# Attention and mixture of experts: a narrower wait for the first gather, token numbers by group, weight parts spread over tiles

## The chip, the cores and the metric

The kernel runs on one core of a Trainium2 chip. The metric is the device time of one execution in microseconds (us). The engines are named as in the profile: PE (TensorE, matrix products), DVE (VectorE), ACT (ScalarE), POOL (GpSimd) and SP (SyncE, which only issues transfers here). Every engine works through its own instructions in order.

## The reference

Attention in blocks of 64 tokens, over a batch of 8, 8 heads, 576 tokens and a head width of 64, gives x with 4608 rows of 512. A router then picks for each row one of 4 groups and one of the group's 4 experts, and the row goes through that expert's two layers (512 to 1024 to 512), scaled by both softmax weights:

```python
attn = softmax(q_c @ k_c.T / sqrt(64))          # each block of 64 tokens
x = (attn @ v_c) as rows of 8 heads x 64         # 4608 x 512
g_idx = argmax(x @ w_group);  g_w = its softmax weight
e_idx = argmax(x @ w_expert[g_idx]);  e_w = its softmax weight
h = maximum(x @ w1[g, e], 0)
out = g_w * e_w * (h @ w2[g, e])
```

## The kernel before, in words

**Attention stage.** The 4608 rows are 36 tiles of 128 tokens, and the tiles form 9 groups of four. A tile t passes through small stages: `stage_b` (scores on PE), `stage_sub` (row maximum and difference on DVE), `stage_exp` (ACT), `stage_ct` (transposes on PE, a copy on ACT), `stage_pv` (weighted sums on PE), `stage_norm` (DVE divides by the row sum and writes the tile of x) and `stage_xt` (transposes of x for the router). In step t of the main loop `stage_b` works on tile t + 1 and `stage_norm` on tile t - 3.

**Routing and scatter.** After the fourth tile of a group, `route` and `place` work out on DVE, in small pieces strewn between the tiles, the expert, the gate (column D + 1 of x) and the row of each token in a table xs in device memory, which has a section for each expert. One tile's position is worked out in each `stage_norm` (`one_scatter`), and POOL scatters that earlier tile into xs (`scatter_x`, line 752). In the same place POOL writes the token numbers of the present tile (column D) with a small copy from a table of constants. A group's x lies in one of four buffers, taken in turn: the buffer called xl holds groups 0, 4 and 8, so group 8's first tile (tile 32) is written over group 4, whose scatters must have landed.

**The first unit.** After group 3 (GC = 3), `choose` picks the expert with most tokens so far. Its first 256 rows are the first unit of the expert stage, and its weights and rows are fetched during the rest of the attention. `first_loads` (F0 to F5) runs on POOL's queue: F0 and F1 load w1 in two parts (w1r), F2 and F3 gather the 256 rows from xs into xg0 (line 812, 128 rows each), F4 and F5 load w2 in two parts (w2r). `prep_static` (P0 to P7) splits w1 into a rounded part, cast by ACT, and the remainder, subtracted by POOL, 512 columns at a time. P0, P1, P4 and P5 read the first part of w1r, the others the second. R0 and R1 let SP load the next weights into w1r, once these have been read.

**What orders the work.** The order within each engine is written out by hand, in three strings of short names: HEAD, EXTRA (what is added at the end of step t) and TAIL (what follows the loop). A recorder keeps for every operation which boxes of memory it reads and writes and derives the waits between engines: a read waits for earlier writes that overlap, a write for earlier reads and writes. A box is one span of bytes on a range of partitions, from the first to the last byte that an operation touches, so gaps within it count as touched. Transfers have lanes with a semaphore each; scatters of group g use lane s(g mod 4), and a wait for one of a group's scatters is a wait for the last of that group recorded so far. All of xs is one box called "xs": the zero fills of `prefill` write it, scatters are recorded as readers of it (so that they don't wait for each other), and the gathers F2 and F3 are recorded as writers. So a gather waits for all scatters recorded before it (at F2 that includes the first two of group 4), the second gather waits for the first, and a later scatter waits for both.

**Expert stage.** After the attention the units of up to 256 tokens go one by one through the two layers in loops of PE work (lines 1094 and 1109 in the profile), with weights reloaded by SP. POOL sends the last group's scatters (line 1589) once all engines have come to the end of the recorded part; then it gathers the second unit.

Of the kernel before, what the change touches and what calls it, by code (L numbers as in the profile page):

```python
# [1 line left out]

# [10 lines left out]
I32 = mybir.dt.int32  # L13
# [6 lines left out]
P = 128  # L20
# [4 lines left out]
D = H * HD  # L25
# [19 lines left out]

HEAD = "q0 I0 q1 V0 q2 q3 V1 q4 q5 V2 I1 G0 Q3 V3 Q4 V4 Q5 V5 Q6"
EXTRA = {3: "C0", 4: "Z0", 5: "Z1", 6: "Z2", 7: "Z3", 8: "Z4",
         24: "F0", 25: "F1", 27: "P0 P1", 28: "F4", 29: "F2 F3", 30: "P2 P3 F5", 31: "P4 P5 P6"}
TAIL = ("b34 n30 s33 c32 m1 p31 m2 e33 x30 b35 n31 s34 m1 c33 P7 p32 m2 e34 x31 36 n32 s35 B0 c34 p33 17 e35 m1 n33 x32 27 W0"
        " p34 c35 n34 B1 m2 W1 x33 W2 p35 n35 m2 x34 X0 x35 X1 m3 R0 R1 37 18 m3 y0 y1 y2 W3 W4 W5 W6 W7 y3 R2 y4 y5 y6 L0 28 m2 m1 L1 m4 H0 y7"  # L50
        " L2 m5 38 D0 L3 m6 H1 L4 D1 L5")

# [64 lines left out]

class Op:
    def __init__(self, eng, fn, lane):
        self.eng, self.fn, self.lane, self.waits, self.inc = eng, fn, lane, [], False  # L120


class Recorder:
# [28 lines left out]
        hi = lo + sum((n - 1) * abs(st) for st, n in dims[1:]) + 1  # L152
        return p0, p0 + dims[0][1], lo * size, hi * size

    def add(self, eng, fn, reads, writes, lane=None, group=None):
        op = Op(eng, fn, lane)
        op.plain = False
        op.at = len(self.ops[eng])
        need = []
        acc = [(a, False) for a in reads] + [(a, True) for a in writes]  # L160
        boxes = []
        for a, w in acc:
            if isinstance(a, tuple):
                key, b, psum = a[0], a[1], False
            else:
                key, b, psum = self.alias.get(a.tensor.name, a.tensor.name), self.box(a), a.space == PSUM
            boxes.append((key, b, w))
            kept = []
            for o, ob, ow in self.hist.setdefault(key, []):
                over = b[0] < ob[1] and ob[0] < b[1] and b[2] < ob[3] and ob[2] < b[3]  # L170
                if over and o is not op:
                    same = o.lane is None and lane is None and o.eng == eng
                    if same and (eng == "tensor" or not ow):
                        pass
                    elif w or ow or (psum and not same):
                        need.append(o)
                if over and w and b[0] <= ob[0] and b[1] >= ob[1] and b[2] <= ob[2] and b[3] >= ob[3] and o is not op:
                    continue
                kept.append((o, ob, ow))
            self.hist[key] = kept  # L180
        for key, b, w in boxes:
            self.hist[key].append((op, b, w))
        if lane is not None:
            n, gen = self.lanes.get(lane, (0, None))
            if group is None or group != gen:
                need += self.last_of(lane)
                self.lanes[lane] = (n + 1, group)
                op.gen = [op]
            else:
                self.lanes[lane] = (n + 1, gen)  # L190
                op.gen = self.live[lane][-1].gen
                op.gen.append(op)
            self.live.setdefault(lane, []).append(op)
            op.number = n + 1
        self.want(op, need)
        self.ops[eng].append(op)
        op.clock = dict(self.seen[eng])
        return op
# [62 lines left out]
    def play(self, name, eng):  # L261
        for op in self.ops[name]:
# [2 lines left out]
                eng.wait_ge(*self.wait(*w))  # L265
            if op.fn is None:
                continue
            z = op.fn(eng)
            for w in last:
                z._wait_ge(*self.wait(*w))  # L270
            if op.lane is not None:
# [19 lines left out]
class Engine:  # L291
    def __init__(self, rec, name):
        self.rec, self.name = rec, name

    def do(self, fn, reads=(), writes=(), lane=None, group=None):
        return self.rec.add(self.name, fn, list(reads), list(writes), lane, group)

    def __getattr__(self, op):
        def f(*args, **kw):
# [6 lines left out]
                writes, reads = [args[0]], aps(args[1:]) + aps(named.values())  # L306
            reads = [a for a in reads if a.space != DRAM]
            writes = [a for a in writes if a.space != DRAM]
            z = self.do(lambda e: getattr(e, op)(*args, **named), reads, writes, lane, group)  # L309
            z.plain = True  # L310
            return z
        return f
# [3 lines left out]
def moe_kernel(tc, qk, v, wgs, w1, w2, cst, out):  # L316
# [4 lines left out]
    with ExitStack() as ctx:  # L321
# [114 lines left out]
        with ExitStack() as c1:  # L436
# [132 lines left out]
            def stage_norm(t):  # L569
# [9 lines left out]
                g, i = divmod(t, NG)  # L579
                if i == 0:  # L580
                    st["x", g] = xl if g % 4 == GL % 4 else xbufs[g % 4 - 1]
                R.gpsimd.tensor_copy(st["x", g][:, i, D:D + 1].bitcast(I32), cs[:, C_TID + t:C_TID + t + 1])
                x = st["x", g][:, i, 0:D]
                R.vector.tensor_tensor(out=x.rearrange("p (h x d) -> p x h d", x=2, d=HD), in0=o[..., 0:HD],
                                        in1=rc.unsqueeze(3).broadcast_to([P, 2, 4, HD]), op=ALU.mult)
# [164 lines left out]
            def scatter_x(pos, g, i):  # L750
                x = st["x", g][:, i, :]
                R.gpsimd.do(lambda e: e.indirect_dma_start(xs, bass.IndirectOffsetOnAxis(ap=pos, axis=0), x, None),  # L752
                            [pos, x, ("xs", (0, 1, 0, 1))], [], "s%d" % (g % 4), g)

            def one_scatter():

# [41 lines left out]
            def first_loads(i):  # L798
# [10 lines left out]
                elif i < NP + 2:  # L809
                    j = i - NP  # L810
                    number(("r", j), xi0[0:1, j:j + 1], E * RE * P)
                    R.gpsimd.do(lambda e: e.dma_start(xg0[:, j, :], xs[ds(st["r", j], P), :]), [], [xg0[:, j, :], ("xs", (0, 1, 0, 1))], "g%d" % j)
                else:
                    load2(R.gpsimd, lambda: st["e0"], i - NP - 2)

# [49 lines left out]

            def prefill(j):
                i = (E * RE, 0, 1, 2, 3)[j]
                R.sync.do(lambda e: e.dma_start(xs[i * P:(i + 1) * P, :], pad), [pad], [("xs", (0, 1, 0, 1))], "z%d" % j)

            def reload(i):  # L870
                (load1, load2)[i // NP](R.sync, 0, i % NP)
# [800 lines left out]
```

## Time and profile before

| | us |
|---|---|
| three runs | 624.0, 624.8, 625.17 |
| median | 624.8 |
| the profiled execution | 627.61 |
| its span, first to last instruction | 626.0 |

| engine | busy us | share of the span |
|---|---|---|
| PE | 583.8 | 93% |
| DVE | 364.3 | 58% |
| ACT | 263.1 | 42% |
| POOL | 161.2 | 26% |

A row of the trace gives the start in us, a length in us, the engine, the line, the operation, what it writes and what it reads with the shapes, and how many alike were merged (x2). Brackets hold the idle time of the engine ahead of it and what ended that time. Operations that go through the recorder all carry line 309, that of the recorder's helper, and are told apart by their operands. SPq is the queue of SP's transfers. PEclk is the granted clock of TensorE as a share of full speed; 0.50 is 1.2 GHz and 1.00 is 2.4 GHz. An indirect transfer of POOL shows there with the time of its issue only; its way to memory is in the chain as a DMA.

### The profile page before, as it was taken

How to read it: one execution, taken by the hardware profiler on the slowest of the kernel's cores; microseconds unless marked ns; L12 is line 12 of the kernel's file. 1: busy time of each engine (PE TensorE's matmuls, PEld its weight loads, DVE VectorE, ACT ScalarE, POOL GpSimd, SP SyncE). 2: the span in 40 equal slices, each digit the busy share in tenths (PEclk: the TensorE clock that was granted, in tenths of full speed). 3: DMA queues.
4: the chain of work that ended last, by engine and by line, in shares of the span. 5: the costliest groups of instructions: out<-in, count | busy, mean ns of one | idle time of the engine just before them, and what ended most of it. 6: DMA issues, size and time to landing. Idle time of an engine off the chain costs nothing.

```text
span 626.0 us, 16004 instructions
## 1 busy us (share of the span) xinstructions
PE 583.8 (93%) x5711; PEld 503.1 (80%) x5712; DVE 364.3 (58%) x688; ACT 263.1 (42%) x367; POOL 161.2 (26%) x279
## 2 busy tenths in 40 slices
PE   6897989957899999989999999999999999999995
PEld 4766767745779799878889899989989988898984
DVE  4586769863876672127497674725525578854311
ACT  2464445743444461125475362625215365552111
POOL 0002324348342311221333212221111124311120
PEclk9798889985999999999999999999999999999999
DMA  8987997729639984115489954451712686931110
GB/s 299 422 278 258 372 363 229 228 77 286 173 108 323 328 300 171 68 30 200 142 298 339 301 191 180 171 206 63 281 50 89 238 317 206 339 102 67 34 38 30
DMA packets 43103, 128.24 MB, mean 205 GB/s; under 512 B 4590, under 2 KB 4974, under 8 KB 41136
## 3 DMA queue, kind: packets, MB, share of 16 engines
q1 hardware_dynamic: 32192, 93.93, 43.4%
q0 software_dynamic: 10864, 33.64, 15.3%
q8 instruction: 35, 0.57, 0.4%
q14 instruction: 12, 0.10, 0.0%
HBM read 106.40 MB, written 21.93 MB: 205 GB/s over the span
## 4 chain that ended last, share of the span: by engine, by line
PE 77%; DMA 10%; DVE 5%; issue 4%; POOL 2%; SPq 1%; ACT 1%; POOLq 0%; ACTq 0%; DVEq 0%
PE banks L1109 29%; PE banks L1094 22%; PE banks L309 14%; PE banks L1078 5%; DMA xs<-xl,pos 3%; DMA w1r<-in_moe_w_dram 2%; DMA xgr<-xs 2%; PE banks L994 2%; DMA out_dram<-xl,io__154 1%; DMA qk<-in_qk_dram 1%; PE banks L1040 1%; PE banks L1063 1%; PE banks L1010 1%; DVE big L309 1%; DVE m L309 1%
## 5 line engine op out<-in xcount | busy, mean ns | idle before, releaser
L1094 PE MATMUL banks<-big,w1h 128*128 128x256 f32 x896 | 128.1, 283 | 1.6 <-issue 1.6
L1094 PEld LDWEIGHTS banks<-big,w1h 128*128 128x128 f32 x896 | 117.3, 192 | 3.0 <-issue 2.0
L1255 ACT ACTIVATE big<-banks 128x512 fp32r<-128x512 f32 x58 | 34.5, 597 | 158.6 <-PE banks L1094 105.3
L1109 PE MATMUL banks<-big,big 128*128 128x512 f32 x360 | 84.6, 393 | 0.0
L1585 POOL DMA_INDIRECT out_dram<-xl,io__154 x37 | 41.1, 1111 | 154.8 <-DVE xl L1321 144.0
L1109 PEld LDWEIGHTS banks<-big,big 128*128 128x128 f32 x360 | 66.5, 188 | 14.4 <-ACT big L1305 0.7
L1354 DVE SCALAR_TENSOR_TENSOR big<-banks,big 128x512 fp32r<-128x512 f32 x54 | 36.1, 687 | 64.5 <-ACT big L1255 64.1
L1094 PE MATMUL banks<-big,w1l 128*128 128x256 f32 x448 | 72.3, 283 | 0.6 <-DVE w1l L1331 0.6
L1109 PE MATMUL banks<-w2h,big 128*128 128x512 f32 x288 | 71.2, 393 | 1.5 <-ACT big L1255 1.4
L1331 DVE TENSOR_TENSOR w1l<-w1r,w1h 128x2048 fp32r<-128x2048 f32 x28 | 63.1, 2290 | 16.1 <-ACT w1h L1242 14.3
L1321 DVE TENSOR_SCALAR xl<-banks,io__154 128x512 f32<-128x512 f32 x33 | 24.7, 748 | 67.5 <-PE banks L1109 66.0
L1109 PEld LDWEIGHTS banks<-w2h,big 128*128 128x128 f32 x288 | 53.1, 188 | 13.0 <-ACT big L1255 1.8
L1094 PEld LDWEIGHTS banks<-big,w1l 128*128 128x128 f32 x448 | 61.9, 192 | 0.8 <-DVE w1l L1331 0.8
L1242 ACT CAST w1h<-w1r 128x2048 fp32r<-128x2048 f32 x28 | 52.1, 1903 | 6.7 <-DMA w1r<-in_moe_w_dram 4.9
L309 PE MATMUL banks<-va,pT 64*64 64x65 f32 x1152 | 30.0, 247 | 13.9 <-DVE x L309 6.9
L309 PEld LDWEIGHTS banks<-va,pT 64*64 64x64 f32 x1152 | 24.2, 154 | 23.2 <-DVE x L309 7.9
L309 PE MATMUL banks<-qk 64*64 64x64 f32 x1152 | 29.4, 233 | 11.6 <-issue 7.8
L309 PEld LDWEIGHTS banks<-qk 64*64 64x64 f32 x1152 | 23.0, 141 | 20.2 <-issue 11.0
L1335 DVE TENSOR_TENSOR w2l<-w2r,w2h 128x1024 fp32r<-128x1024 f32 x32 | 37.1, 1218 | 1.8 <-ACT w2h L1274 1.2
L309 ACT COPY pT<-banks 128x512 f32<-128x512 f32 x36 | 21.1, 585 | 36.4 <-PE banks L309 35.8
L1109 PE MATMUL banks<-w2l,big 128*128 128x512 f32 x144 | 35.6, 389 | 0.0
L752 POOL DMA_INDIRECT xs<-x,pos x24 | 24.8, 1033 | 39.7 <-DVE pos L309 27.0
(218 smaller groups left out, 898.6 us busy)
## 6 DMA issues: line engine op xcount, KB each, us to landing
w1r<-in_moe_w_dram SPq DMA_DIRECT2D x30, 1024.0 KB
w2r<-in_moe_w_dram SPq DMA_DIRECT2D x30, 1024.0 KB
qk<-in_qk_dram SPq DMA_DIRECT2D x15, 1024.0 KB, 15.3
xgr<-xs POOLq DMA_DIRECT2D x38, 257.0 KB, 5.2
va<-in_v_dram SPq DMA_DIRECT2D x24, 390.0 KB
qk<-in_qk_dram SPq DMA_DIRECT2D x6, 512.0 KB, 8.6
w1r<-in_moe_w_dram POOLq DMA_DIRECT2D x2, 1024.0 KB, 9.7
w2r<-in_moe_w_dram POOLq DMA_DIRECT2D x2, 1024.0 KB, 7.2
```

Of the source, the lines that this page charges most:

```text
L309: z = self.do(lambda e: getattr(e, op)(*args, **named), reads, writes, lane, group)
L752: R.gpsimd.do(lambda e: e.indirect_dma_start(xs, bass.IndirectOffsetOnAxis(ap=pos, axis=0), x, None), [pos, x, ("xs", (0, 1, 0, 1))], [], ...
L1078: m = pe.matmul(ph[n], a_[:, c, 0:P], w_[:, c, n * 512:(n + 1) * 512], start=(i == 0), stop=(i == 11))
L1094: m = pe.matmul(ph[f // 2][:, f % 2 * 256:f % 2 * 256 + 256], w_[:, c, f * P:(f + 1) * P], a_[:, c, :], start=(i == 0), stop=(i == 11))
L1109: m = pe.matmul(py[j], a_[:, f, half[j]], w_(b, f), start=(i == 0), stop=(i == 23))
L1242: lambda b, s, j: ac.copy(wt[b][0][:, s], w1r[j]), K1)
L1255: ac.activation(hth()[:, 2 * b:2 * b + 2, :], ph[b].rearrange("p (f t) -> p f t", f=2), AF.Relu).then_inc(S["Ha"], 1)
L1321: return ve.tensor_scalar(out=yb[:, j, :], in0=py[j], scalar1=io_[:, j, 1:2], scalar2=None, op0=ALU.mult)
L1331: lambda b, s, j: ve.tensor_sub(wt[b][1][:, s], w1r[j], wt[b][0][:, s].bitcast(F32)), K1, js)
L1335: m = ve.tensor_sub(wt[b][4 + 2 * j + i], w2r[j][:, 2 * i:2 * i + 2], wt[b][2 + j][:, 2 * i:2 * i + 2].bitcast(F32))
L1354: ve.scalar_tensor_tensor(out=htl()[:, 2 * b:2 * b + 2, :], in0=ph[b].rearrange("p (f t) -> p f t", f=2), scalar=0.0, in1=hth()[:, 2 * b:2 ...
L1585: gp.indirect_dma_start(out, bass.IndirectOffsetOnAxis(ap=io[:, j, 0:1].bitcast(I32), axis=0), yb[:, j, :], None, bounds_check=N - 1, oob_ ...
```

## The change

The first unit's gathers wait only for the scatters of groups 0 to 3 (`after=`), as nothing later writes their rows. For this "xs" is replaced by two names: "zeros", for the fills, which scatters still wait for, and "rows", under which each group's scatters are found. The gathers don't write either, so they don't wait for each other and later scatters don't wait for them. Token numbers are copied by POOL for four tiles at once, at the first tile of a group: 9 copies of 128x4 in place of 36 of 128x1. The box of such a copy goes from column D of the first tile to column D of the fourth, and so covers x of the second to fourth tile. The parts P0 to P7 are dealt out one to a tile in EXTRA and TAIL, and F4 now follows P1. The other lines give each recorded operation its own line number in the profile.

```diff
--- before.py
+++ after.py
@@ -1,3 +1,4 @@
+import sys
 from contextlib import ExitStack
 
 import numpy as np
@@ -45,8 +46,8 @@
 
 HEAD = "q0 I0 q1 V0 q2 q3 V1 q4 q5 V2 I1 G0 Q3 V3 Q4 V4 Q5 V5 Q6"
 EXTRA = {3: "C0", 4: "Z0", 5: "Z1", 6: "Z2", 7: "Z3", 8: "Z4",
-         24: "F0", 25: "F1", 27: "P0 P1", 28: "F4", 29: "F2 F3", 30: "P2 P3 F5", 31: "P4 P5 P6"}
-TAIL = ("b34 n30 s33 c32 m1 p31 m2 e33 x30 b35 n31 s34 m1 c33 P7 p32 m2 e34 x31 36 n32 s35 B0 c34 p33 17 e35 m1 n33 x32 27 W0"
+         24: "F0", 25: "F1", 27: "P0", 28: "P1 F4", 29: "F2 F3 P2", 30: "P3 F5", 31: "P4"}
+TAIL = ("b34 n30 s33 c32 m1 p31 m2 e33 x30 P5 b35 n31 s34 m1 c33 p32 m2 e34 x31 P6 36 n32 s35 B0 c34 p33 17 e35 m1 n33 x32 P7 27 W0"
         " p34 c35 n34 B1 m2 W1 x33 W2 p35 n35 m2 x34 X0 x35 X1 m3 R0 R1 37 18 m3 y0 y1 y2 W3 W4 W5 W6 W7 y3 R2 y4 y5 y6 L0 28 m2 m1 L1 m4 H0 y7"
         " L2 m5 38 D0 L3 m6 H1 L4 D1 L5")
 
@@ -117,7 +118,7 @@
 
 class Op:
     def __init__(self, eng, fn, lane):
-        self.eng, self.fn, self.lane, self.waits, self.inc = eng, fn, lane, [], False
+        self.eng, self.fn, self.lane, self.waits, self.inc, self.stage = eng, fn, lane, [], False, None
 
 
 class Recorder:
@@ -152,11 +153,11 @@
         hi = lo + sum((n - 1) * abs(st) for st, n in dims[1:]) + 1
         return p0, p0 + dims[0][1], lo * size, hi * size
 
-    def add(self, eng, fn, reads, writes, lane=None, group=None):
+    def add(self, eng, fn, reads, writes, lane=None, group=None, after=()):
         op = Op(eng, fn, lane)
         op.plain = False
         op.at = len(self.ops[eng])
-        need = []
+        need = list(after)
         acc = [(a, False) for a in reads] + [(a, True) for a in writes]
         boxes = []
         for a, w in acc:
@@ -265,7 +266,8 @@
                 eng.wait_ge(*self.wait(*w))
             if op.fn is None:
                 continue
-            z = op.fn(eng)
+            with self.tc.nc.source_location(__file__, op.line):
+                z = op.fn(eng)
             for w in last:
                 z._wait_ge(*self.wait(*w))
             if op.lane is not None:
@@ -292,8 +294,10 @@
     def __init__(self, rec, name):
         self.rec, self.name = rec, name
 
-    def do(self, fn, reads=(), writes=(), lane=None, group=None):
-        return self.rec.add(self.name, fn, list(reads), list(writes), lane, group)
+    def do(self, fn, reads=(), writes=(), lane=None, group=None, line=None, after=()):
+        z = self.rec.add(self.name, fn, list(reads), list(writes), lane, group, after)
+        z.line = line or sys._getframe(1).f_lineno
+        return z
 
     def __getattr__(self, op):
         def f(*args, **kw):
@@ -306,7 +310,7 @@
                 writes, reads = [args[0]], aps(args[1:]) + aps(named.values())
             reads = [a for a in reads if a.space != DRAM]
             writes = [a for a in writes if a.space != DRAM]
-            z = self.do(lambda e: getattr(e, op)(*args, **named), reads, writes, lane, group)
+            z = self.do(lambda e: getattr(e, op)(*args, **named), reads, writes, lane, group, sys._getframe(1).f_lineno)
             z.plain = True
             return z
         return f
@@ -579,7 +583,7 @@
                 g, i = divmod(t, NG)
                 if i == 0:
                     st["x", g] = xl if g % 4 == GL % 4 else xbufs[g % 4 - 1]
-                R.gpsimd.tensor_copy(st["x", g][:, i, D:D + 1].bitcast(I32), cs[:, C_TID + t:C_TID + t + 1])
+                    R.gpsimd.tensor_copy(st["x", g][:, :, D].bitcast(I32), cs[:, C_TID + t:C_TID + t + NG])
                 x = st["x", g][:, i, 0:D]
                 R.vector.tensor_tensor(out=x.rearrange("p (h x d) -> p x h d", x=2, d=HD), in0=o[..., 0:HD],
                                         in1=rc.unsqueeze(3).broadcast_to([P, 2, 4, HD]), op=ALU.mult)
@@ -750,7 +754,7 @@
             def scatter_x(pos, g, i):
                 x = st["x", g][:, i, :]
                 R.gpsimd.do(lambda e: e.indirect_dma_start(xs, bass.IndirectOffsetOnAxis(ap=pos, axis=0), x, None),
-                            [pos, x, ("xs", (0, 1, 0, 1))], [], "s%d" % (g % 4), g)
+                            [pos, x, ("zeros", (0, 1, 0, 1)), ("rows", (g, g + 1, 0, 1))], [], "s%d" % (g % 4), g)
 
             def one_scatter():
 
@@ -809,7 +813,8 @@
                 elif i < NP + 2:
                     j = i - NP
                     number(("r", j), xi0[0:1, j:j + 1], E * RE * P)
-                    R.gpsimd.do(lambda e: e.dma_start(xg0[:, j, :], xs[ds(st["r", j], P), :]), [], [xg0[:, j, :], ("xs", (0, 1, 0, 1))], "g%d" % j)
+                    R.gpsimd.do(lambda e: e.dma_start(xg0[:, j, :], xs[ds(st["r", j], P), :]), [], [xg0[:, j, :]], "g%d" % j,
+                                after=[o for o, b, _ in R.hist["rows"] if b[0] <= GC])
                 else:
                     load2(R.gpsimd, lambda: st["e0"], i - NP - 2)
 
@@ -865,7 +870,7 @@
 
             def prefill(j):
                 i = (E * RE, 0, 1, 2, 3)[j]
-                R.sync.do(lambda e: e.dma_start(xs[i * P:(i + 1) * P, :], pad), [pad], [("xs", (0, 1, 0, 1))], "z%d" % j)
+                R.sync.do(lambda e: e.dma_start(xs[i * P:(i + 1) * P, :], pad), [pad], [("zeros", (0, 1, 0, 1))], "z%d" % j)
 
             def reload(i):
                 (load1, load2)[i // NP](R.sync, 0, i % NP)
```

## Rows read from the trace of the kernel before

**Rows 1.** The table of stretches (us; busy time and instructions of each engine, granted clock, DMA).

```profile
100.00:125.00 25.00, 23.67 (x617) 18.17 (x611) 22.71 (x80) 16.53 (x37) 10.61 (x15) 1.00 0.83 257
...
125.00:150.00 25.00, 13.74 (x268) 9.55 (x261) 14.03 (x42) 8.33 (x18) 16.24 (x21) 0.72 0.50 156
...
300.00:626.00 326.00, 318.09 (x1985) 284.65 (x1984) 179.30 (x198) 134.15 (x150) 77.01 (x140) 1.00 0.49 174
...
155.00:156.00 1.00, 1.00 (x23) 0.67 (x25) 0.70 (x4) 1.00 (x4) 0.69 (x2) 0.50 0.97 386
...
54.00:56.00 2.00, 2.00 (x42) 1.55 (x38) 1.09 (x6) 0.85 (x3) 0.00 (x0) 0.50 0.96 209
...
56.00:58.00 2.00, 2.00 (x42) 1.85 (x42) 1.33 (x3) 0.78 (x2) 0.35 (x1) 0.69 0.88 225
```

**Rows 2.** The chain that ended last, 117 to 157 us (start, us, what).

```profile
117.25 8.31 DMA xs<-xl,pos
...
126.24 3.32 DMA xg0r<-xs
...
133.89 1.03 POOL xs L752
...
138.60 7.12 DMA xs<-xl,pos
...
147.97 9.34 PE banks L309 x100
```

**Rows 3.** POOL in order of time (start, us, engine, line, operation; idle before and releaser).

```profile
112.33 2.51 POOL L309 TENSOR_TENSOR w1l<-w1r,w1h 128x512 fp32r<-128x512 f32 x2 [3.19 <-ACT w1h L309]
...
116.14 0.81 POOL L418 DMA_DIRECT2D w2r<-in_moe_w_dram  x1
...
126.24 0.57 POOL L812 DMA_DIRECT2D xg0r<-xs  x1 [7.77 <-DMA xs<-xl,pos]
...
134.93 0.19 POOL L309 CAST x<-cs 128x1 int32<-128x1 f32 x1
...
172.75 0.96 POOL L1589 DMA_INDIRECT xs<-xl,pos  x1 [4.43 <-PE banks L309]
```

**Rows 4.** VectorE (DVE) in order of time.

```profile
100.94 0.24 DVE L309 TENSOR_TENSOR one<-lg,mx 128x80 f32<-128x80 f32 x1
...
113.64 1.29 DVE L309 TENSOR_TENSOR one<-lg,mx 128x80 f32<-128x80 f32 x1
...
118.78 0.17 DVE L309 TENSOR_TENSOR x<-gt 128x4 f32<-128x4 f32 x1
...
124.69 0.69 DVE L309 TENSOR_TENSOR x<-banks,rc 128x512 f32<-128x512 f32 x1
...
135.15 2.43 DVE L309 TENSOR_TENSOR x<-gt 128x4 f32<-128x4 f32 x1 [3.06 <-POOL x L309]
...
141.39 0.23 DVE L309 TENSOR_TENSOR ps<-banks,oh 128x64 f32<-128x64 f32 x1 [1.22 <-PE banks L309]
...
145.81 0.69 DVE L309 TENSOR_TENSOR xl<-banks,rc 128x512 f32<-128x512 f32 x1 [4.06 <-DMA xs<-xl,pos]
...
157.79 0.69 DVE L309 TENSOR_TENSOR xl<-banks,rc 128x512 f32<-128x512 f32 x1
```

**Rows 5.** TensorE (PE) in order of time.

```profile
52.33 0.34 PE L309 MATMUL banks<-qk 64*64 64x64 f32 x6 [1.99 <-issue]
...
126.27 0.70 PE L309 MATMUL banks<-va,pT 64*64 64x65 f32 x32
...
138.24 1.15 PE L309 MATMUL banks<-va,pT 64*64 64x65 f32 x32 [5.85 <-DVE x L309]
```

**Rows 6.** ScalarE (ACT) and SP's DMA queue in order of time.

```profile
111.62 1.14 ACT L309 CAST w1h<-w1r 128x512 fp32r<-128x512 f32 x2
...
142.29 6.89 SPq L412 DMA_DIRECT2D w1r<-in_moe_w_dram  x2
```

## The prediction

> **What bounds the kernel now.** I read the table of stretches first, the chain that ended last second, and then GpSimd (POOL), VectorE (DVE) and TensorE (PE) instruction by instruction between 100 and 160 us. The table [rows 1] parts the kernel in two. From 300 us on PE is busy for 318 of 326 us at full clock: the expert stage is bound by PE, and nothing in this diff touches its code. In the attention stage it is DVE that is nearly full (22.7 of 25 us in 100 to 125). The odd stretch is 125 to 150: PE works 13.7 of 25 us at a mean clock of 0.72, DVE 14 of 25, and DMA halves. Some 12 us of work is missing there, and the question is who holds it up.
>
> The chain [rows 2] names the holder. At 117.25 POOL issues a scatter of tokens (xl to xs), and the chain runs through its landing (8.3 us), then the first unit's gather (3.3 us), then the next scatter at 133.89, then one at 138.60 that takes 7.1 us to land, and then PE work at a slow pace. POOL's own rows [rows 3] say it outright: the gather of line 812 stood 7.77 us for that scatter, that is from 118.47, and the next scatter began at 133.89 only, so POOL, which works in order, was held for 15.4 us. 14.3 us of it is waiting (7.77, then the first gather's landing, then the second's); the rest is the issue of the two gathers.
>
> DVE's rows [rows 4] show the two places where this reaches the attention. The write of the gates of group 6, 0.17 us at 118.78 for the group before, waits 3.06 us at 135.15 for POOL's copy of a token number and then takes 2.43 us. The write of tile 32 into xl waits 4.06 us at 145.81 for the landing of the scatter of 138.60, because xl still holds group 4. PE [rows 5] idles 5.85 us for the first of these; after that its clock falls to 0.50 (1.2 of 2.4 GHz): the mean of 0.72 over 125 to 150 makes 14 us at half, 155 to 156 is still at 0.50 [rows 1], and thirty-two matmuls take 1.15 us where they took 0.70.
>
> **The change part by part.** I set the sum in the profiled execution: it took 627.61 us, its span 626.0, and the median of the runs is 624.8, 0.45% below it. I take the saving off the median.
>
> *The wait of the gather.* The first gather now needs scatters of groups 0 to 3 alone. The last of these stands ahead of P0 on POOL, so it was issued before 112.33 [rows 3], and landing takes 7 to 8.3 us [rows 2]: it is there by 120.6 at the latest, about when the gathers come; the second gather no longer waits for the first, nor the next scatter for both. Removed from POOL: 14.3 us. What that is worth stands with those who waited:
> (a) The gates of group 6: 3.06 us of waiting, and 2.43 less 0.17 for the slow write, 5.3 us.
> (b) Tile 32: 4.05 us. Group 4's last scatter should be issued near 125 (below) and land by 133, while tile 32 comes at about 136.6 (145.81 less 5.3, 4.05, 1.2 and 1.05, plus the 2.4 of (d)), a cover of some 3 us. If that cover is gone, at most these 4.05 us come back.
> (c) The clock. The chain's 9.34 us of PE work from 147.97 ran at half clock; at 0.70 to 1.15 it is 5.7 us, a gain of 3.6. Of the stretch before, DVE's wait of 1.22 us for PE at 141.39 goes as well: 1.2. Together 4.8, and nothing if the clock stays down.
>
> *The low parts, one to a tile.* Eight casts on ACT (0.57 us each) and eight subtractions on POOL (1.25 us each) stay the same [rows 3, 6]; P1 moves one tile on and ahead of F4, P2 comes into the tile of the gathers and right behind them, P3 stays ahead of F5, and P4 to P7 spread over later tiles. On ACT there is room: no cast stands on the chain. On DVE something is won: its operation of 113.64 took 1.29 us instead of 0.24 [rows 4] while POOL ran P0 and P1 back to back, from 112.33 to 114.84; with P0 alone POOL is through at 113.6, so (f) 1.05 us. The two slow rows show that such a DVE operation, both of whose inputs lie in SBUF, stands until POOL's subtraction ends. Between the ends 0 and 1.05 I take 1.05, since DVE starts it after POOL would be through. SP's two reloads of w1 wait for P5 and P7; they were issued from 142.29 over 6.89 us [rows 6], so the second near 149. By the count below P5 ends near 135 and P7 near 143, both earlier, so they cost nothing; DMA is at 0.50 there.
>
> *The token numbers.* 36 copies of 0.19 us on POOL become 9. That is nothing by itself, since POOL idles. But the group's copy spans the rows between the tiles, so DVE, which didn't wait for a copy in its tile writes, now waits for it in the second to fourth tile of each group, and the copy sits in POOL's queue. For groups 0 to 6 POOL is early. For group 7 I count the queue, with 1.2 us for a scatter, 1.25 for a subtraction, 0.8 for a weight load (F4, F5) and 0.75 for a gather [rows 2, 3]: P0 ends 113.6, the scatter in tile 25's step 114.8, P1 (its cast a tile later on ACT, 115.4) 116.65, F4 117.45, scatter 118.65, two gathers 120.15, P2 121.4, scatter 122.6, P3 123.85, F5 124.65, scatter 125.85, copy 126.05. The positions, which DVE works out ahead of each tile, come earlier and don't hold it. DVE writes tile 29 at 124.69 [rows 4], less (f) 123.65. So (d) a new wait of 2.4 us, between 0 (POOL's gaps shorter, the cast earlier) and 4 (register loads before the gathers not hidden). Behind it on DVE stand the maximum and subtraction of tile 32, on PE the weighted sum of tile 30. (e) The copy of group 8 stands behind P6 and a scatter; tile 33 waits 0 to 1.25 us for it, I take 0.6.
> (g) PE then idles some 1.5 us. A pause of 1.99 us before 52.33 [rows 5] was followed by a clock of 0.50 in 54 to 56 and 0.69 in 56 to 58 [rows 1]; these 3 us at half clock cost 1.5, and I take half of it, 0.7.
>
> *The rest.* The line numbers given to instructions add none. The end of attention carries to the end of the kernel: the last scatters (172.75) wait 4.43 us for PE [rows 3], the first unit's and the second's loads follow those, and PE is full after. Sum: 5.3 + 4.05 + 4.8 + 1.05 - 2.4 - 0.6 - 0.7 = 11.5 us, 624.8 to 613.3. With every bound on the good side (no d, e, g) it is 15.2, 609.6; with d 4, e 1.25, g 1.5 and no f it is 7.4, 617.4.
>
> **The rivals.**
> *The clock stays down.* The new wait idles PE at 126 as the old one did at 133, and PE is fed slowly enough that the clock remains at half as it did up to 156 us [rows 1]. For: the pause of 1.99 us was enough. Against: there it was back within some 3 us, since PE was fed. Price: the 4.8 us of (c) and 0.7 more, 613.3 + 5.5 = 618.8.
> *The wait is not lifted.* If the gather is still held (by the lane it shares with group 4, or by another transfer), the same 14.3 us fall on POOL ahead of group 7's copy, for which DVE now waits: the copy comes at 140.4, tile 29 then, tile 32 three tiles of 3.3 us later at 150.3 instead of 145.81, and the 12.0 us from there to tile 35 (157.79) stay: 4.5 us slower, 629.3. It decides from a copy of group 7 later than 126.05 + 11.5 = 137.5. Against: lane counts of groups 0 to 3 are below group 4's, and a wait for a constant count passes once that is reached.
> *Collisions.* Two DVE operations were stopped by POOL's subtractions, for 1.05 and 2.26 us [rows 4]; the forecast has none. One subtraction a tile can meet the routing of groups 5 to 8 in all of them: eight times 1.05 instead of none gives 613.3 + 8.4 = 621.7. Against: each tile has a few such small operations in 3.3 us, most DVE work reads PSUM and ran on undelayed beside POOL. The Trainium skill (SBUF — State Buffer, section SBUF: two separate sides) speaks against the change here: the port pair is an exclusive lock, held for the whole instruction, against DVE operations with two SBUF inputs and also in its two-port modes; by that, up to 8 x 1.25 = 10 us could be lost as an estimate. The two rows agree on the lock, and no row shows a two-port case.
> *Hidden anyway.* Loads, not POOL, would set the end of attention: no change, 624.8. Against: DMA at 0.50 in 125 to 150.
>
> **How the numbers follow.** Forecast 0.70, clock 0.15, collisions 0.06, not lifted 0.06, hidden 0.03. A measurement of this kernel can tell about 0.2% (1.2 us) from no change. Faster: 0.70 + 0.15 + 0.06 = 0.91; same 0.03; slower 0.06. The range runs from every bound good (609.6, set 609.0) over the forecast's bad end to the clock's case (618.8, set 619.0), and leaves out collisions, slower, hidden: 0.15.
>
> **What would show it.** Right: both gathers issued near 119 to 120 without a DMA wait, group 4's last scatter by 126, no DVE wait for a DMA at tile 32, 125 to 150 with DVE above 20 us busy; tile 35 near 146; a DVE wait for POOL's copy at tile 29 of 1 to 4 us. Wrong: a DMA wait at line 813's gathers, a wait at tile 29 above 6 us, a clock of 0.5 for over 5 us, or an expert stage whose start doesn't move with tile 35.

## The result, and the profile of the changed kernel

The changed kernel takes 618.3 us (median of five runs, 616.05 to 620.83), the kernel before 625.17 in the runs beside it (624.0 to 626.44): a ratio of 0.9877, with a 95% interval of 0.9848 to 0.9907. The profiled execution took 618.3 us with a span of 616.7, 9.3 us less than the profiled one of before. The forecast was 613.3 in a range of 609.0 to 619.0, so the first measurement lies 0.7 us inside the range's upper end.

Lines have moved: 756 is the scatter of a tile, 816 the gathers, 586 the copy of token numbers, 438 POOL's subtraction of w1's low part, 588 DVE's write of a tile of x, 577 its reading of the row sums ahead of that, 705 the write of the gates, 662 the difference called `one`, 1594 the last group's scatters; on PE 534 are the scores, 570 the weighted sums, 600 the transposes of a tile of x, 824 the transposes of the first unit. The table of stretches first, against [rows 1]:

```profile
100.00:125.00 25.00, 22.25 (x529) 17.13 (x522) 20.35 (x75) 15.44 (x34) 13.13 (x16) 0.93 0.95 274
125.00:150.00 25.00, 19.18 (x414) 14.50 (x413) 16.92 (x66) 15.65 (x31) 15.94 (x17) 0.96 0.73 205
150.00:175.00 25.00, 24.12 (x168) 20.00 (x167) 18.77 (x74) 12.31 (x16) 10.38 (x8) 0.90 0.47 155
```

The stretch of 125 to 150 has filled up: PE 19.2 us busy for 13.7, DVE 16.9 for 14.0, the clock 0.96 for 0.72, DMA 0.73 for 0.50. But 100 to 125 now holds a stretch at half clock (0.93 for 1.00), and 150 to 175 still does, at 0.90; before, its row was this:

```profile
150.00:175.00 25.00, 22.96 (x224) 20.70 (x225) 16.47 (x69) 13.15 (x24) 11.58 (x14) 0.88 0.68 193
```

POOL's own rows, against [rows 3]:

```profile
117.16 1.00 POOL L756 DMA_INDIRECT xs<-xl,pos  x1 [0.30 <-DVE gt L702]
118.16 1.15 POOL L816 DMA_DIRECT2D xg0r<-xs  x2
121.65 1.27 POOL L438 TENSOR_TENSOR w1l<-w1r,w1h 128x512 fp32r<-128x512 f32 x1 [2.33 <-ACT w1h L437]
...
126.89 1.01 POOL L756 DMA_INDIRECT xs<-xl,pos  x1 [0.30 <-DVE pos L765]
127.89 0.21 POOL L586 CAST x<-cs 128x4 int32<-128x4 f32 x1
...
164.70 0.97 POOL L1594 DMA_INDIRECT xs<-xl,pos  x1 [6.00 <-PE banks L428]
```

Both gathers go out in one piece at 118.16, right behind a scatter, without a wait for a DMA; before, POOL stood 15.4 us here. Group 4's last scatter begins at 126.89, not at 138.60. DVE, against [rows 4]:

```profile
112.93 0.36 DVE L662 TENSOR_TENSOR one<-lg,mx 128x80 f32<-128x80 f32 x1
...
123.27 0.69 DVE L588 TENSOR_TENSOR x<-banks,rc 128x512 f32<-128x512 f32 x1
...
128.13 0.69 DVE L588 TENSOR_TENSOR x<-banks,rc 128x512 f32<-128x512 f32 x1 [1.27 <-POOL x L586]
...
134.51 0.16 DVE L705 TENSOR_TENSOR x<-gt 128x4 f32<-128x4 f32 x1
...
137.94 0.69 DVE L588 TENSOR_TENSOR xl<-banks,rc 128x512 f32<-128x512 f32 x1
...
140.99 0.69 DVE L588 TENSOR_TENSOR xl<-banks,rc 128x512 f32<-128x512 f32 x1 [0.62 <-POOL xl L586]
...
147.79 0.17 DVE L577 TENSOR_SCALAR rc<-banks 128x8 f32<-128x8 f32 x1 [1.49 <-PE banks L824]
...
148.24 0.69 DVE L588 TENSOR_TENSOR xl<-banks,rc 128x512 f32<-128x512 f32 x1
```

These are `one`, tile 28, tile 29 with the new wait for the group's copy, the gates of group 6 (no wait, 0.16 us), tile 32 (no wait for a DMA), tile 33 with its new wait, and tile 35 at 148.24, where it came at 157.79. PE shows where the clock was lost instead, against [rows 5]:

```profile
116.33 0.38 PE L534 MATMUL banks<-qk 64*64 64x64 f32 x9 [2.36 <-issue]
...
118.23 1.15 PE L570 MATMUL banks<-va,pT 64*64 64x65 f32 x32
...
148.99 1.12 PE L600 MATMUL banks<-cs,xl 128*128 128x128 f32 x4 [2.37 <-DVE xl L588]
```

PE paused 2.36 us within a series of matmuls that waits for nothing the profile shows (it calls such time "issue"), and thirty-two matmuls then took 1.15 us, the half-clock price; it idled 2.37 us ahead of tile 35's transposes, and four of them took 1.12 us where four take 0.60 to 0.66 at full clock.

From the starts of the same instructions in both traces, four spans add up to the 9.3 us:

| us | before | after | saved |
|---|---|---|---|
| start to tile 28 (DVE's write) | 121.47 | 123.27 | -1.80 |
| tile 28 to tile 35 | 36.32 | 24.97 | 11.35 |
| tile 35 to the last group's scatters | 14.96 | 16.46 | -1.50 |
| from there to the end of the span | 453.25 | 452.00 | 1.25 |

### The profile page after: what moved, and what is told of

It reads as the page before. It is cut to its first block, busy times and chain, and to the rows that moved or that the text cites. A ratio compares the mean times of both kernels' runs of the same rounds, so it can differ in the third digit from the quotient of the medians.

```text
span 616.7 us, 15975 instructions
## 1 busy us (share of the span) xinstructions
PE 580.7 (94%) x5711; PEld 500.1 (81%) x5712; DVE 361.0 (59%) x688; ACT 263.6 (43%) x367; POOL 157.6 (26%) x252
## 4 chain that ended last, share of the span: by engine, by line
PE 82%; DMA 6%; issue 4%; DVE 4%; POOL 1%; ACT 1%; SPq 1%; DVEq 0%; ACTq 0%; POOLq 0%
PE banks L1114 29%; PE banks L1099 24%; PE banks L1083 5%; PE banks L570 4%; PE banks L534 3%; PE banks L600 3%; PE banks L558 3%; DMA w1r<-in_moe_w_dram 2%; PE banks L999 2%; PE banks L620 2%; DMA qk<-in_qk_dram 1%; PE banks L1045 1%; DMA xs<-x,pos 1%; PE banks L1068 1%; PE banks L1015 1%
## 5 line engine op out<-in xcount | busy, mean ns | idle before, releaser
L1336 DVE TENSOR_TENSOR w1l<-w1r,w1h 128x2048 fp32r<-128x2048 f32 x28 | 63.1, 2290 | 16.1 <-ACT w1h L1247 14.3
L1114 PE MATMUL banks<-w2l,big 128*128 128x512 f32 x144 | 35.6, 390 | 0.0
L1584 POOL COPY in__155<-xgr 128x2 int32<-128x2 int32 x22 | 10.8, 490 | 88.9 <-PE banks L999 75.4
L1340 DVE TENSOR_TENSOR big<-w2r,big 128x1024 fp32r<-128x1024 f32 x28 | 32.5, 1220 | 1.5 <-ACT big L1251 1.5
```

The source lines that it names most:

```text
L1114: m = pe.matmul(py[j], a_[:, f, half[j]], w_(b, f), start=(i == 0), stop=(i == 23))
L1336: lambda b, s, j: ve.tensor_sub(wt[b][1][:, s], w1r[j], wt[b][0][:, s].bitcast(F32)), K1, js)
L1340: m = ve.tensor_sub(wt[b][4 + 2 * j + i], w2r[j][:, 2 * i:2 * i + 2], wt[b][2 + j][:, 2 * i:2 * i + 2].bitcast(F32))
```

## The experiments

Theory: the narrow wait carries the whole gain, the other two parts move nothing by themselves, and what the forecast lacks is the clock. Rivals: a part of the gain is the line numbers'; the new copies' waits eat a part of it; the spread subtractions carry a part of it; the late end of attention is set at tile 35, by something the change brought. The kernels ran in three sets, each on a chip of its own beside the kernel before: line numbers, wait, copies, and wait with spread in the first (before: 623.97 us); spread, wait with copies, the change again and the exact boxes in the second (624.69); the rest in the third (618.62). All of them carry the change's line numbers. First each part alone.

### Line numbers alone

```diff
+            with self.tc.nc.source_location(__file__, op.line):
+                z = op.fn(eng)
```

> The kernel before with one line number per recorded operation and nothing else. Both theories: no change, 625 us within 0.2%, and a second profile of before. If the profile of before (627.61) was at the slow end of its executions, this one shows a span nearer 623.5, with the same two waits (gates of group 6, tile 32) but a shorter stay at half clock. If line numbers matter, it moves by over 1.2 us.

622.22 us (618.96 to 626.18), ratio 0.9966 (0.9941 to 0.9992). No engine has another instruction, so a third of a per cent is what two builds of the same work can differ by here; the 0.2% that the prediction named as the bound of a measurement was too fine. The two kernels below that keep the old wait carry the line numbers too and are not faster than before (1.0033 and 1.0002), so no part of the gain is seen to be theirs. Of the kernel before, 22 of 23 runs lie between 617.93 and 626.27 in this set. The waits of before stand in DVE's rows of this kernel:

```profile
132.89 2.43 DVE L705 TENSOR_TENSOR x<-gt 128x4 f32<-128x4 f32 x1 [1.90 <-POOL x L586]
...
144.26 0.69 DVE L588 TENSOR_TENSOR xl<-banks,rc 128x512 f32<-128x512 f32 x1 [4.76 <-DMA xs<-xl,pos]
```

### The narrow wait alone

(The zero fills write "zeros" too, as in the change.)

```diff
-                            [pos, x, ("xs", (0, 1, 0, 1))], [], "s%d" % (g % 4), g)
+                            [pos, x, ("zeros", (0, 1, 0, 1)), ("rows", (g, g + 1, 0, 1))], [], "s%d" % (g % 4), g)
...
-                    R.gpsimd.do(..., [], [xg0[:, j, :], ("xs", (0, 1, 0, 1))], "g%d" % j)
+                    R.gpsimd.do(..., [], [xg0[:, j, :]], "g%d" % j,
+                                after=[o for o, b, _ in R.hist["rows"] if b[0] <= GC])
```

> Only the gather's wait is narrowed; copies and subtractions as before. Theory A (the wait carries nearly all of the gain): by POOL's queue the last scatter of group 4 is issued near 126.4 and lands by 134, before tile 32, and no DVE wait for POOL's copy at tile 29 is left: 616.5 to 618.5 us, as fast as the whole change. Rival B (without the spreading, P4 to P6 in a row hold POOL and the gain is halved): 620.5 to 622.5 us.

613.81 us (612.31 to 616.35), ratio 0.9833 (0.9807 to 0.9859): the whole gain, not less than with the rest, and 2.7 us below the better of the two times expected. Beside the kernel with line numbers alone it is 8.4 us. With the subtractions still bunched, POOL no longer waits, and P4 to P6 now run into DVE's routing. POOL's row, DVE's rows and PE's row of this kernel, one after the other:

```profile
126.12 3.72 POOL L438 TENSOR_TENSOR w1l<-w1r,w1h 128x512 fp32r<-128x512 f32 x3
```

```profile
126.38 3.57 DVE L662 TENSOR_TENSOR one<-lg,mx 128x80 f32<-128x80 f32 x1
129.87 0.23 DVE L664 TENSOR_TENSOR ls<-lg,mx 128x80 f32<-128x80 f32 x1
```

```profile
131.51 0.70 PE L570 MATMUL banks<-va,pT 64*64 64x65 f32 x32 [3.36 <-DVE x L588]
```

The operation, 0.24 us long where nothing stops it, starts 0.26 us after the first of three subtractions and ends as the third does (126.12 + 3.72 = 129.84; the next row of DVE starts at 129.87), and PE idles 3.36 us for it. Yet tile 35 comes at 145.90.

### The grouped copies alone

```diff
-                R.gpsimd.tensor_copy(st["x", g][:, i, D:D + 1].bitcast(I32), cs[:, C_TID + t:C_TID + t + 1])
...
+                    R.gpsimd.tensor_copy(st["x", g][:, :, D].bitcast(I32), cs[:, C_TID + t:C_TID + t + NG])
```

> Only the copies are grouped; the gather waits as before. Theory A: group 7's copy stands behind the held gathers and the scatter of tile 28's step, at about 139.6, and DVE stands at tile 29 from 124.7 until then; tile 32 comes near 150 instead of 145.8: 629 us (627 to 631), slower. Rival (the copies are off every path): 625 us.

625.89 us (622.25 to 627.74), ratio 1.0033 (1.0005 to 1.0061); 3.7 us above the kernel with line numbers alone. This is the prediction's slow rival in a kernel of its own: the old wait on POOL, with group 7's copy behind it. The wait came as expected, the time did not (629). DVE's row of tile 29, then PE's next one:

```profile
135.72 0.69 DVE L588 TENSOR_TENSOR x<-banks,rc 128x512 f32<-128x512 f32 x1 [15.39 <-POOL x L586]
```

```profile
136.46 1.15 PE L570 MATMUL banks<-va,pT 64*64 64x65 f32 x32 [13.91 <-DVE x L588]
```

Tile 29 waits 15.39 us, PE idles 13.91. It costs so little more than before because the waits at the gates and at tile 32 are then over (tile 32 at 147.72 without a wait): one long wait takes the place of two short ones.

### The spread subtractions alone

```diff
-         24: "F0", 25: "F1", 27: "P0 P1", 28: "F4", 29: "F2 F3", 30: "P2 P3 F5", 31: "P4 P5 P6"}
+         24: "F0", 25: "F1", 27: "P0", 28: "P1 F4", 29: "F2 F3 P2", 30: "P3 F5", 31: "P4"}
```

(and P5 to P7 in TAIL, as in the change)

> Only the subtractions are spread; the gather waits and the copies go as before. Theory A (POOL is held by the gathers, and the scatter of tile 28's step has the same work ahead of it): 622 to 624 us, no change. Rival (spreading is worth its relief on DVE even so): 620 to 621 us.

624.12 us (622.77 to 628.44) beside 624.69, ratio 1.0002 (0.9974 to 1.003): nothing that could be measured. `one` takes 0.36 us here too, but another operation of the routing (0.17 us elsewhere) now stands until a subtraction of POOL (128.61 to 129.89) is through, and both old waits are there in DVE's rows:

```profile
128.42 1.50 DVE L703 TENSOR_TENSOR cum<-cum 128x16 bf16<-128x16 bf16 x1
...
133.17 1.22 DVE L705 TENSOR_TENSOR x<-gt 128x4 f32<-128x4 f32 x1 [3.10 <-POOL x L586]
...
141.76 0.69 DVE L588 TENSOR_TENSOR xl<-banks,rc 128x512 f32<-128x512 f32 x1 [3.19 <-DMA xs<-xl,pos]
```

### The narrow wait with one other part

The change with the copies put back to one a tile (the reverse of the diff of the grouped copies):

> The whole change without the grouping of copies. Theory A (DVE's waits for a copy, 1.27 us at tile 29 and 0.62 at tile 33, lie on the path): 616.4 us, 1.9 faster than the change. Rival (PE, not DVE, sets the pace there, or the clock falls all the same): 618.3 us, no change against it.

613.45 us (612.89 to 616.47), ratio 0.982 (0.9798 to 0.9843). No DVE operation waits for POOL, and none is stopped by it for more than 0.12 us (`one`, 0.36). Both times expected (616.4 and 618.3) were too high.

The change with the subtractions put back to their old places (the reverse of the diff of the spread):

> The narrow wait and the grouped copies, with the subtractions where they were before. Theory A (by POOL's queue group 7's copy comes at 126, DVE waits 2.9 us at tile 29, but its next routing operation, which stood 3.57 us behind P4 to P6 with the wait alone, comes when POOL is nearly through, so most of the wait is hidden): 614 to 615.5 us. Rival (the waits for copies add in full): 617 to 618 us, as the whole change.

618.04 us (613.33 to 619.42), ratio 0.9888 (0.9843 to 0.9933), the rival's time. Tile 29 waits 3.02 us for the copy, `one` takes 1.29 us at 113.13 and 1.55 at 129.37. This and the first measurement of the change stand 3 to 4 us above the two versions with single copies (0.9888 and 0.9877 of 624 against 0.9833 and 0.982). Are the copies' false waits the reason?

### The change again, and with exact boxes

> The kernel after the change, unaltered, beside the others of this job. If grouping the copies costs what the last runs suggest (the kernel without it at 613.45, the change at 618.3), it is again 616.5 to 619 us here; if that gap was a difference between jobs or a pause in one profile, it comes to 613 to 615 us.

614.65 us (613.06 to 618.13), ratio 0.9854 (0.9811 to 0.9897). That is 10 us below the kernel before by the medians of this set, and within the 613 to 615 us expected if the gap does not repeat.

The copy recorded as the four columns it writes, so that tiles 29 and 33 have no reason to wait for it:

```diff
-                    R.gpsimd.tensor_copy(st["x", g][:, :, D].bitcast(I32), cs[:, C_TID + t:C_TID + t + NG])
+                    x4 = st["x", g]
+                    R.gpsimd.do(lambda e: e.tensor_copy(x4[:, :, D].bitcast(I32), cs[:, C_TID + t:C_TID + t + NG]),
+                                [cs[:, C_TID + t:C_TID + t + NG]], [x4[:, k, D:D + 1] for k in range(NG)])
```

> The change with the grouped copy recorded as writing four boxes of one column each, as it really does, so that DVE's tile writes no longer wait for it; the nine copies, the narrow wait and the spreading stay. Theory A (the false wait of DVE for POOL's copy is what the grouping costs): 613.5 us, as without the grouping, and no DVE wait for POOL at tiles 29 and 33. Rival (it is the copy's place in POOL's queue or PE's pauses that cost): 616.5 to 619 us, as the change.

616.36 us (612.41 to 619.88), ratio 0.9879 (0.9837 to 0.9921). The waits at both tiles are gone from its trace, and no gain shows (614.65 for the change beside it, each with a spread of 5 to 7 us). So the false wait of 1.3 to 2.2 us is not shown to be what the change loses.

### Side by side once more, and with PE kept busy

In the third set the kernel before took 618.62 us (617.35 to 621.52). The change a third time:

> The change unaltered, for the comparison on one chip with the version whose token copies stay single and with both under six extra matmuls. In its profile TensorE idled 2.37 us before tile 35's transposes and then ran at half clock (1.2 GHz) for some 6 to 10 us. If the grouped copies have a cost that repeats (tile 29's wait of 1.3 to 2.2 us and tile 33's of 0.6 to 0.7), it stands 2 to 3 us above the version with single copies; if the 1 to 4 us that lay between them before were the spread of the executions, the two lie within 1.2 us. 615 to 618 us at a kernel before of 624.5.

609.84 us (608.12 to 610.96), ratio 0.9847 (0.9822 to 0.9873).

The version with single copies beside it:

> Narrow wait and subtractions one to a tile, token copies single as before: the version that measured a ratio of 0.982. If single copies are worth something, 613 to 614 us, 2 to 3 below the change on the same chip; if not, 615 to 617, within 1.2 us of it. No wait of DVE for GpSimd at tiles 29 and 33 in either case.

610.83 us (608.85 to 614.74), ratio 0.9862 (0.9835 to 0.989). On one chip the two are 1.0 us apart, the grouped copies ahead, within the 1.2 us expected if the gap was the spread of the executions; with the six matmuls of the next pair it is the other way round, by 2.9 us. So the 3 to 4 us of the first sets does not repeat on one chip. Yet over all sets the kernels with the narrow wait lie at 0.9847 to 0.9888 with grouped copies and at 0.982 to 0.9862 with single ones: a cost of some 2 us is neither shown nor excluded.

Six matmuls between the first unit's first transposes and tile 35's, in the change and in the version with single copies:

```diff
-         " p34 c35 n34 B1 m2 W1 x33 W2 p35 n35 m2 x34 X0 x35 X1 m3 ...
+         " p34 c35 n34 B1 m2 W1 x33 W2 p35 n35 m2 x34 X0 u6 x35 X1 m3 ...
```

> The change plus six matmuls of 512 columns (some 0.4 us each) on TensorE between the first unit's first transposes and tile 35's, where it idled 2.3 to 2.4 us. Nothing of the result depends on them. If the half clock that follows that idle time is what costs, the clock stays at 2.4 GHz over tile 35 and the gap from tile 35 to the last scatters shrinks from 16.5 to some 15 us: 1.5 us below the change. If the idle time itself costs (the late release of tile 35's row sums), no change, within 1.2 us. If they delay tile 35's transposes, 1 to 2.4 us above it.

> Single copies, narrow wait, spread subtractions, plus the same six matmuls. In this version's profile TensorE did not idle 2.4 us at tile 35, only some 0.5 us. So the matmuls fill nothing: if the clock is what costs elsewhere, no gain here, and up to 2.4 us more where they push tile 35's transposes back; within 1.2 us if they fall beside other waits. If it shows the 2.4 us of idle time after all, the idle time belongs to the execution and not to the version, and the matmuls gain as they do in the change.

611.17 us (606.98 to 613.74), ratio 0.9882 (0.985 to 0.9913), and 608.29 us (606.96 to 610.69), ratio 0.9828 (0.98 to 0.9855): one slower, one faster than the same kernel without them, by 1.3 and 2.5 us. I settle nothing from that, since neither profile has the idle time that they were to fill. PE's rows of the change with the six:

```profile
137.32 1.48 PE L859 MATMUL banks<-ones 128*128 128x512 bf16 x6
138.64 0.60 PE L600 MATMUL banks<-cs,xl 128*128 128x128 f32 x4
```

They take 1.48 us together (0.25 each, for the 0.4 that I had expected), and tile 35's transposes follow right behind at full clock. More can be learnt from the change itself in its third profile, where the same program shows no late release either (DVE's row sums of tile 35, then PE's transposes of it):

```profile
142.96 0.17 DVE L577 TENSOR_SCALAR rc<-banks 128x8 f32<-128x8 f32 x1 [0.53 <-PE banks L570]
```

```profile
144.15 0.66 PE L600 MATMUL banks<-cs,xl 128*128 128x128 f32 x4 [0.51 <-DVE xl L588]
```

In its second profile, as in the first, the row sums of tile 35 came late, and PE idled for them (DVE's and PE's rows of the second):

```profile
141.14 0.17 DVE L577 TENSOR_SCALAR rc<-banks 128x8 f32<-128x8 f32 x1 [1.45 <-PE banks L824]
```

```profile
142.33 0.66 PE L600 MATMUL banks<-cs,xl 128*128 128x128 f32 x4 [2.34 <-DVE xl L588]
```

So one program has it in some executions and not in others. The spread alone, with the old wait and single copies, has it too (PE's row of that kernel):

```profile
153.82 1.10 PE L600 MATMUL banks<-cs,xl 128*128 128x128 f32 x4 [2.48 <-DVE xl L588]
```

So it does not need the change. Whether the change makes it more frequent is open: leaving out the six matmuls, four of five profiles with the narrow wait and grouped copies have it, and none of three with the narrow wait and single copies. In all five profiles that have it the clock is at half behind it (143 to 154 us in the second profile of the change), and from tile 35 to the last scatters the three profiles of the change take 16.46, 18.48 and 14.90 us. The five profiles with an idle time of 2.0 to 2.5 us there need 16.46 to 18.48 us; the seven others without the six matmuls need 14.90 to 15.02.

### All profiles in one table

From the same instructions as in the table above, us:

| | tile 28 | 28 to 35 | 35 to last scatters | 28 to end |
|---|---|---|---|---|
| before | 121.47 | 36.32 | 14.96 | 504.53 |
| line numbers alone | 119.95 | 35.33 | 14.96 | 503.05 |
| spread alone | 117.86 | 35.21 | 16.90 | 503.64 |
| grouped copies alone | 117.12 | 38.82 | 14.94 | 507.38 |
| wait alone | 119.99 | 25.91 | 15.01 | 492.31 |
| wait and spread | 121.58 | 25.25 | 15.02 | 493.22 |
| wait and spread, again | 116.98 | 25.14 | 15.01 | 496.12 |
| wait and copies | 120.96 | 27.56 | 16.89 | 495.24 |
| the change | 123.27 | 24.97 | 16.46 | 493.43 |
| the change, second | 114.97 | 26.62 | 18.48 | 496.63 |
| the change, third | 116.94 | 26.46 | 14.90 | 492.36 |
| exact boxes | 118.57 | 25.47 | 16.68 | 492.23 |
| the change, six matmuls | 114.06 | 23.19 | 15.48 | 491.24 |
| wait and spread, six matmuls | 115.57 | 26.85 | 15.56 | 493.43 |

Every version with the narrow wait needs 23.2 to 27.6 us from tile 28 to 35, every one without it 35.2 to 38.8. Tile 28 itself, ahead of which the change does next to nothing, comes anywhere from 114.1 to 123.3. The mean from 28 to the end is 503.7 for the three with the old wait and single copies and 493.9 for the eight with the narrow wait and no extra matmuls: 9.8 us.

## Why the prediction was right, and which term was off

The forecast (613.3, faster) is borne out in kind, and its range holds the measurement near the slow end. The change measured 0.9877, 0.9854 and 0.9847, which of 624.8 us is 617.1, 615.7 and 615.2: a saving of 7.7 to 9.6 us where the sum said 11.5.

Of the signs that it named, the gathers (118.16, without a wait for a DMA), the scatter (126.89), tile 32 and tile 29 came as said. Tile 35 came at 148.24 for "near 146", and DVE is busy for 16.9 us between 125 and 150, not for more than 20. One sign of being wrong came true: a clock of 0.5 for over 5 us, from 148 to 154.

**The wait (a, b).** Right in place. Gates: 0.16 us without a wait, for 3.06 and 2.43 before. Tile 32: no wait for a DMA. Both gathers went out at 118.16, and group 4's last scatter began at 126.89, said to be "near 125"; the cover at tile 32 (137.94) held. That the wait alone gives 0.9833 and the other parts alone 1.0033 and 1.0002 shows that (a), (b) and what follows from them are the whole gain.

**The new waits (d, e).** Tile 29 waited 1.27, 2.22 and 1.66 us in the three profiles, with 2.4 foretold and 0 to 4 as bounds; tile 33 waited 0.62, 0.71 and 0.72 with 0.6 foretold. The queue counted instruction by instruction had the copy done at 126.05; it was done at 128.10 (127.89 + 0.21), in an execution in which tile 28 came 2.9 us later than the count had it (123.27 for 121.47 - 1.05). As time they cost nothing that could be measured: between tile 28 and 35 the kernel with exact boxes needs 25.47 us, the change 24.97 to 26.62. But the spread of the runs would hide a cost of that size.

**DVE's relief (f), a term that the runs do not show.** The step was "so (f) 1.05 us". The operation took 0.36 us instead of 1.29 (0.24 was foretold), but no time is seen to follow: the spread alone, with its operation at 0.36 us too, measures 1.0002, and with the narrow wait the spread takes 613.45 us for 613.81. But 1.05 us is a ratio of 0.9983, within the interval of the spread alone, so it is not excluded either. In the changed kernel tile 28 came 1.80 us later, behind PE's pause of 2.36 us.

**The clock (c, g), a term that came in part.** The step was "a gain of 3.6 ... Together 4.8, and nothing if the clock stays down", less 0.7 for (g). Summed over windows of 1 us, the kernel before spends 20 us between 100 and 180 at half clock, the change 10, 14 and 10 in its three profiles. In the first, none of it lies between tile 28 and 35, neither where it was before nor where (g) had it (PE idled 0.37 us for tile 29, not 1.5): the clock stayed up there. But it fell with the pauses that end at 116.33 and at 148.99, and the second of these gave 1.50 us back behind tile 35. In the other two profiles it fell behind a pause between tile 29 and 30 (2.48 and 1.82 us of "issue"), and once more later on.

**The sum.** Its terms between tile 28 and 35 (all but f) make 5.3 + 4.05 + 4.8 - 2.4 - 0.6 - 0.7 = 10.45 us. The first profile gained 11.35 there; with the new waits as measured (1.27 and 0.62) and without (g) the terms make 12.26, so 0.9 us of them is not accounted for. Over all profiles it is 9.7 (35.6, the mean of the three with the old wait and single copies, less 25.9, the mean of the eight with the narrow wait). Of the 11.5 us, then, the 1.05 of (f) is not seen, and some 0.75 is missing between tile 28 and 35. Why is argued, not shown: the clock and PE's pauses are the likely cause, as the two later profiles have half clock there. The rest of the distance to 618.3 in the first measurement is no larger than the differences between sets: the two later ones put the change at 615 to 616 on the scale of 624.8.

**The rivals.** The slow one, DVE behind group 7's copy at tile 29, was priced 4.5 us over before; built, it came 2.1 over before by its ratio (0.0033 of 624) and 3.7 over the kernel with line numbers alone, with a wait of 15.39 us where 14.3 had been put on POOL. Collisions didn't occur in the change beyond 0.12 us (`one` at 0.36), but the narrow wait without the spread has one of 3.57 us, and there is no measurable difference between the two (0.9833 and 0.982). The Trainium skill (SBUF — State Buffer, section SBUF: two separate sides) calls the port pair an exclusive lock, under which the other side blocks for the whole instruction; the trace agrees, and the 3.57 us shows more: DVE's operation did not get in between three subtractions in a row. The 10 us that the prediction worked out as an upper estimate had no counterpart in the change. Of "the clock stays down" half came true by length (10 to 14 of 20 us at half clock), but at other places and behind other pauses than it had.

**Open.** Why PE pauses where the profile shows no wait was not tested. The traces point to instructions that come late. One of the DMA queues on the profile's page is named "instruction" (packets, MB, share of 16 engines):

```profile
q8 instruction: 35, 0.57, 0.4%
```

In the fourteen traces PE has 34 pauses of "issue" of 0.15 us or more between 100 and 140 us, and 32 of them end 1.2 to 2.4 us after the end of a 16 KB packet of that queue (the one that ends at 116.33: a packet from 112.59 to 113.94). Why the row sums of tile 35 come late in some executions only is open too. In the first profile ACT's copy of tile 34's transposes came late together with them:

```profile
147.91 0.58 ACT L601 COPY xT<-banks 128x512 f32<-128x512 f32 x1 [1.08 <-PE banks L824]
```

PE's semaphore stood still there from 144.22 to 147.77 and then rose three times within 0.12 us; so PE's results were late, not DVE.

## What to carry to other kernels

A wait that a tracker draws too wide costs more where an in-order queue stands behind it than at the waiting instruction: look for what that queue still owes the other engines (here a token number and the freeing of a buffer), and price those. Measure an edit from the last instruction ahead of it to the end, in several executions: here the time up to tile 28 moved by 9 us between profiles, as much as the edit was worth. A stall that is removed gives back its clock only as far as nothing else lowers it.

## What the runs showed of the hardware that I had not expected

PE pauses inside a series of matmuls, at the same place of the program, for a length that changes with the execution. After the twenty-third of a certain series of thirty-two score matmuls (at 116.33 in the first profile) the change shows 2.36, 0.18 and 0.72 us of "issue" in its three profiles, the single-copy version 1.38 and 1.64 in its two. Behind the 2.36 and the 1.38 us the clock fell to its lower level (1.2 GHz) for 3 us; behind the 1.64, the 0.72 and the 0.18 us it did not. So the length of the pause alone doesn't tell. In the third profile of the change it fell once more at 135.6, behind idle times of no more than 0.41 and 0.72 us. These pauses lie ahead of tile 28 and are a part of the 9 us by which it moves; the rest of that was not looked into.

A DVE operation with two SBUF inputs can be held by several GpSimd operations in a row, not by one alone: 3.57 us behind three of 1.24 each.

Taking away a wait of 1.3 to 2.2 us on DVE (the exact boxes) gave nothing that could be measured, and a stall of 3.57 us (the wait alone, against wait and spread) cost nothing that could be measured: tile 28 to 35 took 25.91 us with it and 25.25 without.
